# The two products of a level of the attention's inversion handed out as two pieces, with the shares per slot raised by 1.12

## The chip, the cores and the metric

The kernel runs on one core of one Trainium2 chip. The metric is the device time of one execution in microseconds; the median over the runs counts.

## The reference, cut to what matters

Inputs are q, k, v of shape (4, 8, 768, 48), beta of shape (4, 8, 768) and the weights of two mixtures. Three parts follow one another:

```python
# attention with a delta rule, per batch and head, over t = 0 .. 767
y[t] = q[t] @ state
state = state + beta[t] * outer(kn[t], v[t] - state.T @ kn[t])
# first mixture: x is y as 3072 tokens x 384
h = x @ w_in                      # 384 x 2048
x2 = maximum(0.01 * h, h) @ w_out # 2048 x 384
# second mixture, 8 experts, P by 8 rounds of normalising rows and columns
out = sum_e P[:, e] * (maximum(x2 @ w1[e], 0) @ w2[e])   # 384 x 1024 x 384
```

## The kernel before, in words

**Staging.** The 768 positions are cut into 6 steps (t) of 128 positions; a step holds 4 batches (b) of 8 heads. Within a step the recurrence is solved in closed form: part1 normalises k, transposes it and forms the lower triangular matrix of a step (nh and nl are its high and low half in fp16); solve inverts the 32 x 32 diagonal blocks for all batches at once on VectorE (16 x 16 for steps 0 and 1, named in SMALL); part2(t, b) joins the blocks level by level to the inverse of 128 x 128, refines it, and applies it to v and to the state. The first mixture (main_a) then takes the 512 tokens of a step, and the second mixture begins when all six steps are through.

**A level.** For s in (32, 64), and 16 ahead of them in steps 0 and 1, the loop in part2 (L275 on) does: 8 small products of nh and a half of u into a PSUM bank (L284), copies of the result into p by ScalarE (L287), 8 products of x with p (L290) and, for s over 16, 8 products of p with x (L294) into two more banks, and copies of these back into u and x (L297, L300). The second products wait for the copies of the first. A level ends with a yield.

**The order of the work.** part1, solve and part2 are generators; what stands between two yields is a piece. Two queues hold them: bgq has the threads part2(t, b), bgs has part1 and solve. `pump` takes one piece from the next active thread, round robin; the end of a thread counts as one more unit. Main work is also a generator: main_a yields after each third of a first product (L503, three matmuls of 512 columns) and after each of three output chunks of a second product (L555, three matmuls). Each yield is a slot: step 0 has 120, the others 96. At each slot `spend` adds the share of RATES0 (step 0, six equal stretches of slots) or RATES (steps 1 to 4, four stretches) to a credit and pumps one piece for each whole credit: the first number of a triple is for bgq, the second for bgs, the third for pieces of convert, which rewrites the weights of the first mixture. If nothing can be pumped (a part2 waits until solve of its step is done), the credit is cut to 1 and the slot passes.

```python
                ru, rs, rc = rates[n * len(rates) // total]
                bgq.spend(ru, 3)
                bgs.spend(rs, 1)
```

A thread (t, b) starts when (t, b - 2), or (t - 1, b + 2) for b below 2, has ended, so at most two part2 run side by side. Ahead of the first item of the next step, need_x1 pumps bgq until all four threads of that step are through, without main work between, and then transposes their y into x1. Step 0 runs its first LEAD = 4 items on batches 0 and 1 alone, and need_x1 has a stop for batches 2 and 3 after three of them.

**The start.** part2(0, 0) and part2(0, 1) run before main_a, in 14 rounds: one piece of each of the two, one of part1(1) and one of convert. What is left of the three after 14 rounds is run one after the other.

```python
        for _ in range(14):
            run(a0, 1)
            run(a1, 1)
            with tc.issue_after(solved[0].ins):
                run(p1_1, 1)
            run(cv_gen, 1)
        run(a0)
        run(a1)
```

The pieces of part2 in order: two for the products of q and k (m, L256), one for the blocks (L271), one per level, two for the refinement (p, L309 and L311), two for its product with x (u, L321), one for the state's part (ks, L329), w (L337), and y with the new state (L343, L346, L354). The build orders each engine's instructions by their place in the program and by when it takes them to be ready, so the order on an engine can differ from that of the code. Pools: bg has three PSUM banks for the pieces, po three for the second product, ph two for the first.

Of the kernel before, what the change touches and what calls it, by code (L numbers as in the profile page):

```python
# [41 lines left out]

STIR = (145, 20)

RATES0 = ((0.65, 0.3, 0.1), (0.7, 0.5, 0), (0.7, 0.45, 0), (1.05, 0.8, 0.4), (0.7, 0.35, 0), (1.05, 0, 0))
RATES = ((0.7, 0.5, 0), (0.7, 0.5, 0), (0.7, 0.5, 0), (0.7, 0.7, 0))


@with_exitstack
def delta_moe_kernel(ctx: ExitStack, tc: tile.TileContext, k_l, v_l, q_l, beta_l, wa_in, wg, wc, out):  # L50
# [67 lines left out]
    def bank(name):  # L118
        if early is not None and early:
            early[0] += 1  # L120
            i = early[0] % 6
            if i >= 3:
                return po_p.tile([128, 512], F32, tag=f"po{i - 3}", name=name)
        return bg_p.tile([128, 512], F32, tag="bg", name=name)
# [92 lines left out]
    def solve(t):  # L217
        size = 16 if t in SMALL else 32
        nd = 32 // size

        def blocks(x):
            return x[:, 0:nd * size * 33].rearrange("p (d r) -> p d r", d=nd)[:, :, 0:size * 32].rearrange(
                "p d (c i) -> p d c i", c=size)[:, :, :, 0:size]

        ld = a1_p.tile([128, 1056], F16, tag="ld", name="ld")
        dve.transpose(out=ld[:, 0:1024], in_=a_d.rearrange("p a b -> p (a b)"))
        xs = a1_p.tile([128, 1056], F32, tag="xs", name="xs")
        pool.memset(xs, 0.0)
        pool.memset(xs[:, 0:1024:33], 1.0)
        ldb, xsb = blocks(ld), blocks(xs)  # L230
        yield
        for j in range(size - 1):
            m = size - 1 - j
            tm = a1_p.tile([128, 1024], F32, tag="tm", name="tm")
            tv = tm[:, 0:nd * (j + 1) * m].rearrange("p (d c i) -> p d c i", d=nd, c=j + 1)
            xv = xsb[:, :, 0:j + 1, j + 1:]
            dve.tensor_tensor(out=tv, in0=ldb[:, :, j:j + 1, j + 1:].to_broadcast([128, nd, j + 1, m]),  # L237
                              in1=xsb[:, :, 0:j + 1, j:j + 1].to_broadcast([128, nd, j + 1, m]), op=ALU.mult)
            dve.tensor_tensor(out=xv, in0=xv, in1=tv, op=ALU.subtract)
            if j % 2 == 1:  # L240
                yield
        xt = a1_p.tile([128, 32, B * H], F32, tag="tm", name="xt")
        solved.append(dve.transpose(out=xt.rearrange("p a b -> p (a b)"), in_=xs[:, 0:1024]))
        xt_of[t] = xt
        done.add(("xt", t))
        yield

    def part2(t, b):
# [26 lines left out]
        for s in (16, 32, 64) if t in SMALL else (32, 64):  # L275
            pt = p1[b % 2]
            nb = C // (2 * s)

            def half(ap, odd):
                return ap.rearrange("p h (n two s) -> p h n two s", two=2, s=s)[:, :, :, odd, :]  # L280

            ps = bank("l_ps").rearrange("p (h n s) -> p h n s", h=H, n=nb)
            for h in range(H):
                marks.append(pe.matmul(out=ps[:, h], lhsT=nh[:, h, :], rhs=half(u, 1)[:, h], start=True, stop=True))  # L284
            for i in range(nb):
                o = 2 * s * i
                act.activation(out=pt[o:o + s, :, o + s:o + 2 * s], in_=ps[o:o + s, :, i, :], func=ACTF.Copy)  # L287
            ps = bank("l_ps").rearrange("p (h n s) -> p h n s", h=H, n=nb)
            for h in range(H):
                pe.matmul(out=ps[:, h], lhsT=x[:, h, :], rhs=half(pt, 1)[:, h], start=True, stop=True)  # L290
            if s > 16:
                ps2 = bank("l_ps").rearrange("p (h n s) -> p h n s", h=H, n=nb)
                for h in range(H):
                    pe.matmul(out=ps2[:, h], lhsT=pt[:, h, :], rhs=half(x, 0)[:, h], start=True, stop=True)  # L294
            for i in range(nb):
                o = 2 * s * i
                act.activation(out=u[o:o + s, :, o + s:o + 2 * s], in_=ps[o:o + s, :, i, :],  # L297
                               func=ACTF.Copy, scale=-1.0)
                if s > 16:
                    act.activation(out=x[o + s:o + 2 * s, :, o:o + s], in_=ps2[o + s:o + 2 * s, :, i, :],  # L300
                                   func=ACTF.Copy, scale=-1.0)
            if s == 16:
                dve.transpose(out=x.rearrange("p a b -> p (a b)"), in_=u.rearrange("p a b -> p (a b)"))
            yield
# [187 lines left out]
    def step_items(t):  # L492
        n = LEAD if t == 0 else 0
        return ([(t, f, 0, 2) for f in range(n)] + [(t, f, 0, B) for f in range(n, NF1)]
                + [(t, f, 2, B) for f in range(n)])
# [80 lines left out]
    if True:  # L576
# [7 lines left out]
        def load_part2(t, b):  # L584
            def run():
                if (t, b) not in vq:
                    load_vq(t, b)
                yield from part2(t, b)
            return run
# [57 lines left out]
        for t in range(NT - 1):  # L647
            add_step2(t + 1)
            if t + 2 < NT:
                tt = t + 2  # L650
                bgs.add(("p1", tt), lambda tt=tt: part1(tt), after=[("s", t + 1)] + [("p2", t, b) for b in range(B)])
                bgs.add(("s", tt), lambda tt=tt: solve(tt), after=[("p1", tt)] + [("p2", t + 1, b) for b in range(B)])
            rates = RATES if t else RATES0
            total = 6 * len(step_items(t))
# [429 lines left out]
```

## Time and profile before

| what | value |
|---|---|
| runs | 2474.03, 2477.55, 2491.28 us; median 2477.55 us |
| profiled execution | 2491.82 us, its span 2489.8 us |
| mean granted clock of TensorE | 0.963 |
| TensorE matmul, weight loads | 95%, 84% of the span |
| VectorE, ScalarE, GpSimd | 51%, 47%, 38% of the span |

Times within the execution count from the span's start. The x1 transposes, which end a step's attention, stand at 112 and 163 us (the two halves of step 0) and at 315, 449, 588, 724 and 843 us (steps 1 to 5); the second mixture begins at about 945 us. PE is TensorE, PEld its weight loads, DVE VectorE, ACT ScalarE, POOL GpSimd, SP the engine that issues most DMAs. Ends of matmuls are modelled; a row's bracket gives the idle time of the engine before it and who ended it.

### The profile page before, as it was taken

The numbers are of one execution on the slowest core, as the hardware profiler recorded it, in microseconds if no ns is written. First come the engines' busy times: TensorE is split into PE (matmuls) and PEld (weight loads), VectorE is DVE, ScalarE is ACT, GpSimd is POOL, SyncE is SP. The second block draws the span as 40 slices with busy tenths as digits, with TensorE's granted clock in tenths as the row PEclk, the third lists the DMA queues.
The fourth block names the chain that finished last, engine by engine and source line by source line (L and its number), as shares of the span: only waits on it lengthen the run. The fifth ranks groups of instructions, "written<-read, shape, count | busy, mean of one in ns | idle before, by whom it ended". The sixth has DMA issues, their size and how long they took to land.

```text
span 2489.8 us, 35427 instructions
## 1 busy us (share of the span) xinstructions
PE 2374.4 (95%) x13836; PEld 2087.3 (84%) x13836; DVE 1263.4 (51%) x2320; ACT 1162.8 (47%) x2121; POOL 937.5 (38%) x966
## 2 busy tenths in 40 slices
PE   6788899999999999999999999999999999999999
PEld 5776677877877777899999999999999999999998
DVE  8567846446362357644444454444444544444444
ACT  6887666564654544433333344333333443333332
POOL 6435312132322213444434444444444443444441
PEclk7689999989899999999999999999999999999999
DMA  3355552424233552111111131111111311111111
GB/s 117 122 172 181 185 174 94 142 92 142 82 126 129 165 174 76 51 51 46 49 46 51 52 102 51 46 51 51 49 48 51 96 45 51 51 51 46 50 51 38
DMA packets 108695, 214.83 MB, mean 86 GB/s; under 512 B 11504, under 2 KB 79728, under 8 KB 108528
## 3 DMA queue, kind: packets, MB, share of 16 engines
q1 hardware_dynamic: 108528, 212.58, 27.5%
q8 instruction: 108, 1.77, 0.3%
q14 instruction: 59, 0.48, 0.1%
HBM read 190.43 MB, written 22.02 MB: 85 GB/s over the span
## 4 chain that ended last, share of the span: by engine, by line
PE 77%; ACT 10%; DVE 7%; issue 3%; DMA 2%; POOL 2%; SPq 0%; ACTq 0%; POOLq 0%; DVEq 0%
PE ye L964 32%; PE ph L880 13%; PE w L880 5%; PE y L880 5%; PE z L880 5%; PE ph L503 4%; PE po L555 4%; PE y_ps L346 2%; ACT x L271 2%; PE w_ps L337 2%; ACT a_d L205 1%; ACT p L287 1%; PE g_ps L189 1%; ACT u L297 1%; DVE tm L237 1%
## 5 line engine op out<-in xcount | busy, mean ns | idle before, releaser
L745 POOL TENSOR_TENSOR w2l<-stg,w2h 128x768 fp32r<-128x768 f32 x96 | 182.2, 1898 | 454.2 <-ACT w2h L744 454.2
L734 POOL TENSOR_TENSOR w1l<-stg,w1h 128x384 fp32r<-128x384 f32 x192 | 271.4, 1436 | 184.7 <-ACT w1h L733 167.2
L977 DVE SCALAR_TENSOR_TENSOR acc<-ye,pm,acc 128x384 f32<-128x384 f32 x168 | 103.5, 616 | 435.4 <-PE ye L964 435.4
L731 POOL TENSOR_TENSOR stg<-stg 128x128 f32<-128x128 f32 x384 | 209.0, 565 | 305.5 <-DMA stg<-wc 284.5
L890 ACT ACTIVATE xc<-ph 128x512 f32<-128x512 f32 x96 | 57.5, 599 | 448.5 <-PE ph L880 345.3
L555 PE MATMUL po<-gh,w 128*128 128x512 f32 (+1 forms) x600 | 217.3, 406 | 2.9 <-ACT gh L543 2.8
L880 PE MATMUL ph<-xoh,w1h 128*128 128x512 f32 x480 | 193.1, 402 | 4.7 <-DVE q L895 3.1
L503 PE MATMUL ph<-x1h,w 128*128 128x512 f32 (+1 forms) x600 | 186.7, 418 | 8.9 <-DVE leak L541 4.4
L895 DVE TENSOR_TENSOR q<-q,ph 128x512 f32<-128x512 f32 x192 | 132.2, 688 | 121.8 <-PE ph L880 121.8
L880 PE MATMUL ph<-xoh,w1l 128*128 128x512 f32 x480 | 188.1, 392 | 0.0
L880 PE MATMUL ph<-xol,w1h 128*128 128x512 f32 x480 | 187.7, 391 | 0.0
L733 ACT ACTIVATE w1h<-stg 128x384 fp32r<-128x384 f32 x192 | 121.1, 680 | 116.8 <-DMA stg<-wc 82.7
L541 DVE TENSOR_TENSOR leak<-leak,ph 128x512 f32<-128x512 f32 (+1 forms) x100 | 66.3, 663 | 165.7 <-ACT leak L540 165.5
L503 PEld LDWEIGHTS ph<-x1h,w 128*128 128x128 f32 x600 | 113.2, 202 | 32.5 <-DMA w<-wa_scratch 5.9
L555 PEld LDWEIGHTS po<-gh,w 128*128 128x128 f32 x600 | 115.4, 196 | 25.6 <-ACT gh L543 5.5
L545 POOL TENSOR_TENSOR gl<-leak,gh 128x512 fp32r<-128x512 f32 x48 | 62.1, 1294 | 192.4 <-ACT gh L543 174.7
L555 PE MATMUL po<-gl,w 128*128 128x512 f32 (+1 forms) x300 | 120.2, 401 | 3.8 <-POOL gl L545 2.3
L895 DVE TENSOR_TENSOR c<-xc,y 128x512 f32<-128x512 f32 x96 | 66.0, 688 | 106.2 <-PE y L880 83.1
L880 PEld LDWEIGHTS ph<-xoh,w1h 128*128 128x128 f32 x480 | 90.2, 188 | 34.4 <-DVE h31l L909 6.8
L880 PEld LDWEIGHTS ph<-xoh,w1l 128*128 128x128 f32 x480 | 90.2, 188 | 19.5
L540 ACT ACTIVATE leak<-ph 128x512 f32<-128x512 f32 (+1 forms) x100 | 57.8, 578 | 96.5 <-PE ph L503 93.8
L880 PEld LDWEIGHTS ph<-xol,w1h 128*128 128x128 f32 x480 | 90.3, 188 | 14.2
(316 smaller groups left out, 6683.7 us busy)
## 6 DMA issues: line engine op xcount, KB each, us to landing
w<-wa_scratch SPq DMA_DIRECT2D x100, 768.0 KB, 4.3
stg<-wc SPq DMA_DIRECT2D x192, 384.0 KB, 3.3
raw<-wa SPq DMA_DIRECT2D x48, 256.0 KB, 3.0
wa_scratch<-cvp SPq DMA_DIRECT2D x48, 256.0 KB, 2.5
stg<-x_scratch SPq DMA_DIRECT2D x10, 768.0 KB, 4.7
q<-q_l SPq DMA_DIRECT2D x24, 256.0 KB, 2.7
v<-v_l SPq DMA_DIRECT2D x24, 192.0 KB, 2.4
x_scratch<-x2o SPq DMA_DIRECT2D x18, 256.0 KB, 3.8
```

What stands on the lines that cost most here:

```text
L503: pe.matmul(out=ps, lhsT=wt[:, c * 128:(c + 1) * 128], rhs=xx[:, c], start=(n == 0), stop=(n == 3 * KD - 1))
L541: dve.tensor_tensor(out=g, in0=g, in1=ps, op=ALU.max)
L545: (dve if t in (0, 1, NT - 1) else pool).tensor_tensor(out=gl, in0=g, in1=fr(gh), op=ALU.subtract)
L555: pe.matmul(out=po[c][:, cols], lhsT=wt[:, DM + c * 128:DM + (c + 1) * 128], rhs=xx, start=(i == 1 and m == 0), stop=(i == n and m == 2), ...
L731: pool.tensor_tensor(out=s[:, o], in0=s[:, x], in1=s[:, y], op=op)
L733: ordered(act.activation(out=hi[:, j], in_=s[:, i], func=ACTF.Copy))
L734: pool.tensor_tensor(out=lo[:, j], in0=s[:, i], in1=fr(hi[:, j]), op=ALU.subtract)
L745: pool.tensor_tensor(out=lo, in0=s, in1=fr(hi), op=ALU.subtract)
L880: ordered(pe.matmul(out=ps, lhsT=w[:, a], rhs=x[:, b].rearrange("p s k -> p (s k)"), start=first, stop=i == 2 and (a, b) == terms[-1], ski ...
L895: ordered(dve.tensor_tensor(out=c, in0=x, in1=y, op=op))
L964: ordered(pe.matmul(out=ps[:, 0:DM], lhsT=xx[:, o:o + 128], rhs=wt, start=(f == 0 and i == 0), stop=(f == NF2 - 1 and i == 2), skip_group_ ...
L977: dve.scalar_tensor_tensor(out=a, in0=y, scalar=pm[:, t * B + b, e:e + 1], in1=a, op0=ALU.mult, op1=ALU.add)
```

## The change

The level's loop gets a yield between the copies of the first product and the second products, and the first numbers of the triples are raised (0.65 to 0.72, 0.7 to 0.78, 1.05 to 1.15); the shares of bgs and convert stay. Nothing else changes: the same instructions with the same operands.

```diff
-RATES0 = ((0.65, 0.3, 0.1), (0.7, 0.5, 0), (0.7, 0.45, 0), (1.05, 0.8, 0.4), (0.7, 0.35, 0), (1.05, 0, 0))
-RATES = ((0.7, 0.5, 0), (0.7, 0.5, 0), (0.7, 0.5, 0), (0.7, 0.7, 0))
+RATES0 = ((0.72, 0.3, 0.1), (0.78, 0.5, 0), (0.78, 0.45, 0), (1.15, 0.8, 0.4), (0.78, 0.35, 0), (1.15, 0, 0))
+RATES = ((0.78, 0.5, 0), (0.78, 0.5, 0), (0.78, 0.5, 0), (0.78, 0.7, 0))
@@ -285,6 +285,7 @@
             for i in range(nb):
                 o = 2 * s * i
                 act.activation(out=pt[o:o + s, :, o + s:o + 2 * s], in_=ps[o:o + s, :, i, :], func=ACTF.Copy)
+            yield
             ps = bank("l_ps").rearrange("p (h n s) -> p h n s", h=H, n=nb)
             for h in range(H):
                 pe.matmul(out=ps[:, h], lhsT=x[:, h, :], rhs=half(pt, 1)[:, h], start=True, stop=True)
```

## Rows read from the trace of the kernel before

**Rows 1.** The page, busy us (share of the span) xinstructions:
```profile
PE 2374.4 (95%) x13836; PEld 2087.3 (84%) x13836; DVE 1263.4 (51%) x2320; ACT 1162.8 (47%) x2121; POOL 937.5 (38%) x966
```

**Rows 2.** Stretches; busy us (instructions) by engine, granted clock, DMA share, GB/s:
```profile
0.00:164.00 164.00, 121.09 (x984) 107.82 (x985) 117.46 (x299) 118.66 (x264) 78.09 (x97) 0.70 0.44 140
164.00:317.00 153.00, 127.64 (x1009) 105.12 (x1010) 119.03 (x267) 112.92 (x259) 62.75 (x73) 0.91 0.55 177
317.00:591.00 274.00, 256.32 (x1914) 211.99 (x1913) 146.78 (x327) 161.94 (x290) 67.54 (x62) 0.94 0.36 120
591.00:845.00 254.00, 240.96 (x1801) 198.93 (x1800) 96.39 (x192) 136.29 (x251) 69.50 (x62) 0.95 0.36 117
...
945.00:2489.80 1544.80, 1537.23 (x7754) 1395.24 (x7752) 729.07 (x1155) 585.74 (x982) 637.34 (x652) 1.00 0.19 53
```

**Rows 3.** Waits of TensorE in 0:164, then in 164:845 (us, times, longest):
```profile
PE l_ps L290 <- ACT p L287: 9.6, 10, 3.4
...
PE l_ps L290 <- ACT p L287: 18.3, 28, 1.8
```

**Rows 4.** Timeline 480.75 to 485.55, two levels of step 3's threads:
```profile
480.75 0.84 PE L503 MATMUL ph<-x1l,w 128*128 128x512 f32 x3
...
481.43 0.41 PE L284 MATMUL l_ps<-u,nh 128*128 128x64 f16 x8
...
481.67 0.95 PE L503 MATMUL ph<-x1h,w 128*128 128x512 f32 x3
...
482.45 0.40 PE L555 MATMUL po<-gh,w 128*128 128x512 f32 x1
...
482.69 0.41 PE L290 MATMUL l_ps<-p,x 128*128 128x64 f16 x8
...
483.17 0.40 PE L284 MATMUL l_ps<-u,nh 128*128 128x64 f16 x8
...
483.40 0.48 PE L555 MATMUL po<-gl,w 128*128 128x512 f32 x1
...
483.72 0.62 PE L555 MATMUL po<-gh,w 128*128 128x512 f32 x2
...
484.41 0.62 PE L555 MATMUL po<-gh,w 128*128 128x512 f32 x2
484.74 0.76 ACT L287 ACTIVATE p<-l_ps 32x256 f16<-32x256 f32 x2
...
485.55 0.39 PE L290 MATMUL l_ps<-p,x 128*128 128x64 f16 x8 [0.52 <-ACT p L287]
```

**Rows 5.** Timeline of the start, ACT's part of part1(1) and a conversion's pass:
```profile
99.63 1.06 ACT L198 ACTIVATE nh<-a 128x1024 f16<-128x1024 f32 x1
100.59 2.57 ACT L205 ACTIVATE a_d<-a 32x256 f16<-32x256 f32 x4
...
103.18 0.42 ACT L459 ACTIVATE cvp<-cva 128x256 fp32r<-128x256 f32 x1
```

**Rows 6.** Timeline of TensorE at the end of step 1's main loop:
```profile
436.70 1.88 PE L337 MATMUL w_ps<-v,uc 128*128 128x48 f32 x16
...
441.66 1.03 PE L343 MATMUL y_ps<-state,q 112*128 112x96 f32 x8
...
445.10 1.06 PE L343 MATMUL y_ps<-state,q 112*128 112x96 f32 x8
...
448.56 1.04 PE L481 MATMUL x_ps<-ident,y 128*128 128x128 f32 x8
```

**Rows 7.** Stretches at that end and around a fall of the clock, columns as in rows 2:
```profile
436.00:449.00 13.00, 13.00 (x110) 12.61 (x109) 8.04 (x22) 3.95 (x8) 0.00 (x0) 1.00 0.41 132
...
503.80:517.70 13.90, 11.96 (x93) 10.28 (x91) 8.17 (x15) 12.90 (x21) 7.15 (x6) 1.00 0.22 72
517.70:531.40 13.70, 13.70 (x59) 12.83 (x58) 2.85 (x10) 4.92 (x8) 3.94 (x3) 0.50 0.29 91
531.40:545.10 13.70, 13.68 (x103) 11.47 (x104) 4.79 (x13) 6.68 (x12) 4.26 (x4) 1.00 0.23 78
```

## The prediction

> **What bounds the kernel now.** I read the page's busy shares first, then the stretches, then TensorE's waits, and last the timeline of one level. TensorE is busy 95% of the span and no other engine over 51% [rows 1], so the time is TensorE's work plus its idle time. The stretches [rows 2] show where it idles: from 945 us on, in the last mixture, 1537.23 of 1544.80 us are busy at full clock, and nothing of the change is there. Ahead of 845 us, where attention and first mixture are mixed, 164.00 − 121.09 = 42.9 us are idle in 0:164 (before x1 of step 0 is whole), 25.4 in 164:317, 17.7 in 317:591 and 13.0 in 591:845. The change lives in these 99 us.
>
> The waits [rows 3] put a name on part of them. The second product of a level (L290) waits for the copies p of the first (L287): 9.6 us (10 waits) in 0:164 and 18.3 us (28 waits) in 164:845, together 27.9. The timeline [rows 4] shows one wait whole: two L555 begin at 484.41 and need 2 × 0.227 us, so L290 could begin at 484.86; it begins at 485.55, when ACT's L287 ends. Lost are 0.69 us where the row books 0.52, because matmul ends are modelled late. (0.227 is the pitch: three L503 follow 0.68 us after three others all through this loop, as from 480.75 to 481.43.) With 0.16 us more for each, the 38 waits are 27.9 + 6.1 = 34 us: 18.3 + 4.5 = 23 in 164:845 and 9.6 + 1.6 = 11 before.
>
> The same rows show that TensorE's order isn't the order of the code: between L284 and L290 of one piece stand three L503 and one L555. The build's ordering by priority puts main matmuls there already, but too few: the first product at 481.43 lets L290 go at 482.69 (1.3 us), the one at 483.17 only at 485.55 (2.4 us; its copies start at 484.74, since ACT has others to do first).
>
> **The change, part by part.** *The split.* No instruction is added or removed. The later half gets a later place in the hand-out, so a lower priority than the main matmuls of the slots in between. Following the credits through the code: of the 56 levels (8 threads of steps 0 and 1 with three, 16 with two) 6 lie in the start and 50 in the main loops. In 45 of these, two or three slots and one piece of the other thread now stand between the halves, in 3 one slot, in 2 none. A slot is three matmuls, 0.68 us [rows 4]. The other thread's half adds 0.23 us (L284, 483.17 to 483.40) or about twice that (L290 and L294). So 1.6 to 2.5 us stand where 1.3 to 2.4 are needed. Bounds in 164:845: 0 to −23 us. I take three quarters, −17, since the needed time comes near the given one only where ACT is queued.
>
> *The start (0:164).* Here there is little to fill with. Threads (0,0) and (0,1) had 13 pieces and an end, just the 14 rounds; they now have 16, so w and y (L337, L346) fall behind the loop. The other users of a round keep their count: the rest of part1(1) is out by round 10, where the threads were at their u pieces and are now at p; three more conversions stand ahead of w. If all of that delays the chain, part1's last piece costs ACT 1.06 + 2.57 us and three conversions of some four passes of 0.42 us another 5 [rows 5]: +9 us together. On the other side all 11 us of waits could go. The start is one chain of dependent pieces, at a mean clock of 0.70 [rows 2], so a wait removed there mostly becomes the next wait: −11 to +9, and I take 0. The DMAs that these pieces issue (raw, cvp on SP) keep their order, and no queue gets a new wait ahead of them.
>
> *Rates.* A thread of step 2 and later has 15 units instead of 13 (1.15 times), of steps 0 and 1 17 instead of 14 (1.21); the shares rise by 1.10 to 1.12. So a slot gets a little less of the attention done. solve(2) ends at slot 33 of step 1 instead of 27, as its predecessors end at slots 96 and 97 instead of 87 and 89 of step 0. What is undone when the next step's x1 is needed is pumped in one go: for step 2 nine pieces (u0, two u1, ks, w and y of both threads) where there were two y, for steps 3 to 5 three or four (of w, w, y, y) where there were none, none and one; at step 0's first stop 20 instead of 15. The end of step 1's loop shows such a burst as it is now [rows 6]: y, state, y, state follow from 441.66 to 448.56 without a main matmul and without a wait, then x1, and TensorE is busy 13.00 of 13.00 us at full clock [rows 7]. Bounds: 0, if the longer ones run like that, to +27 (the slow rival's price, below). I take +0.5 us for each of four, for y that waits on the copy of w: +2.
>
> *Closer pieces, more changes of kind.* Every other pair of dependent pieces comes 1/0.70 − 1/0.78 = 0.15 slot nearer, 0.1 us. And where a small product ends and main matmuls resume, the first takes 0.32 us (483.40 to 483.72) instead of 0.227. If all 50 halves come to stand alone that is 50 × 0.09 = 4.5 us; at least 0, since many have main matmuls around them already. With the 0.1 us on some other waits I take +3 (bounds 0 to +10). PSUM gains room: a level held three of three bg banks in one piece, now one and then two. The buffer of p is held longer, but belongs to one thread until that ends.
>
> Sum: −17 + 0 + 2 + 3 = −12 us on the profiled execution (2491.82 us around a span of 2489.8), so 2480 there. That execution stands at the upper edge of the runs (2474.03 to 2491.28); against their median 2477.55 the forecast is 2466 us.
>
> **The rivals.**
> *The clock comes back too.* In 164:845 the missing clock of [rows 2] adds up to 2 × (0.09 × 153 + 0.06 × 274 + 0.05 × 254) = 86 us at half rate, worth 43 us. The fall at 517.7 us [rows 7] follows a stretch with 11.96 of 13.90 us busy; in the stretch after the half-rate one, 13.68 of 13.70 are busy and the clock is 1.00. Denser halves would then pay twice: all 34 us of waits and a tenth of the clock (4), less 4 of price, make −34, 2443 us. The Trainium skill ("TensorE: Matmul & The Clock Gate", Part 1: The HAM clock gate) has the slow clock as the default that activity lifts; the trace agrees, in that this fall follows idle time. Against the rival: only a part of those waits lies near a fall of the clock, and the start is a chain.
> *Nothing moves.* The second half is taken as soon as it is ready all the same, or the wait goes to the next reader of u and x (p, L309). Then ±4 us: 2477. For it: the fill of [rows 4]. Against it: 28 waits that the present order does leave.
> *Slower: the bursts fall to half clock.* w and y are products of 48 columns; four step ends now have w, w, y, y back to back, where the y alone took 6.9 us [rows 6]. If each leaves a half-rate stretch as long as that of [rows 7], 13.7 us, it costs 6.9 us, four of them 27; with 5 us won by the split and 3 lost by closer pieces that is +25: 2502. From the third step end on (17/6.9 = 2.5) it eats the gain. Against it: 436:449, with two w and two y in it, ran at 1.00 [rows 7].
>
> **How the numbers follow.** Forecast 0.50 (own range 2453 to 2479), clock 0.20, nothing 0.15, bursts 0.15. About 1% (25 us) is what a measurement of this kernel can tell from no change. Faster by over 1% (below 2453): the clock case and the forecast's edge, 0.20; slower by over 1% (above 2502): the worse half of the bursts and a little of the start's, 0.09; the rest, 0.71, within. The range leaves out the better half of the clock case and the worse half of the bursts: 2443 to 2495.
>
> **What would show it.** Right: L290's wait for L287 falls from 18.3 to some 5 us in 164:845, with two main slots between L284 and L290; the last mixture keeps its 1545 us; x1 of steps 1 to 5 comes 2 to 4 us earlier per step. The start is right if 0:164 keeps its length within 5 us. The burst term is wrong if the granted clock falls around the step ends, or if L503 waits for x1 there. The forecast as a whole is wrong if L290's wait shrinks and TensorE's idle time ahead of 845 us does not.

## The result, and the profile after

The changed kernel takes 2502.78 us (median of 6 runs, 2501.51 to 2507.79) against 2487.95 (6 runs of before on that chip, 2474.03 to 2491.28): the ratio of the two means is 1.0076, 95% interval 1.0051 to 1.0102. It is slower by three quarters of a per cent, where 2466 us were forecast, and lies above the forecast's range. The profiled execution took 2501.51 us around a span of 2499.8, so 10 us of span more than the one of before [rows 1]. That is half of the 19 us between the means of the runs: before's profiled execution is slower than each of its six runs, and after's is its fastest. The stages below explain these 10 us; what the other runs add stands with the experiments.

The page of the kernel after, TensorE's busy row and the row of its granted clock:

```profile
PE 2388.0 (96%) x13836; PEld 2088.5 (84%) x13836; DVE 1266.0 (51%) x2320; ACT 1158.1 (46%) x2121; POOL 937.3 (37%) x966
PEclk7588899998989999999999999999999999999999
```

TensorE has the same 13836 matmuls and is busy for 13.6 us longer. Its idle time is span less busy: 2499.8 − 2388.0 = 111.8 us after and 2489.8 − 2374.4 = 115.4 before. So the change did take idle time away, and the span still grew. What else makes a matmul long is its clock: the mean granted clock was 0.963 before and 0.960 after, and (1 − clock) × span, the cost of running part of the span at half rate, is 92.1 and 100.0 us. So 10.0 = −3.6 (idle) + 7.9 (clock) + 5.7 (the rest, by subtraction: matmuls that got longer at the same clock, as no run shows apart).

The stretches of the kernel after, which answer to [rows 2] (columns as there):

```profile
0.00:166.00 166.00, 124.65 (x985) 109.23 (x985) 114.91 (x293) 116.76 (x259) 76.15 (x93) 0.70 0.40 127
166.00:332.00 166.00, 138.60 (x990) 111.60 (x989) 124.80 (x271) 115.32 (x264) 67.52 (x79) 0.86 0.53 173
332.00:604.00 272.00, 256.01 (x1931) 208.76 (x1930) 148.42 (x329) 160.36 (x294) 65.73 (x60) 0.94 0.37 122
604.00:854.00 250.00, 239.33 (x1801) 195.12 (x1800) 93.28 (x192) 132.60 (x245) 69.53 (x62) 0.96 0.36 119
954.00:2499.80 1545.80, 1538.26 (x7755) 1395.63 (x7753) 729.96 (x1155) 586.00 (x982) 636.18 (x652) 1.00 0.19 53
```

Most of the clock's loss is in the second stretch: 166:332 ran at a clock of 0.86 for 990 matmuls, where 164:317 had 0.91 for nearly as many. The last mixture is what it was (1545.8 us against 1544.8). Cut at the products of x1, the stages are: the start (until x1 of step 0 is made whole) 162.7 us before and 164.7 after; the first loop (from there to x1 of step 1) 152.5 and 165.8; the later loops (to x1 of step 5) 527.6 and 521.6. So +2.0, +13.3, −6.0, and +0.7 behind. Nearly all of the loss is in the first loop; the later loops, where most of the split's gain was expected, did gain, but 6 us and not most of 17.

The waits of TensorE in 0:166, the first row, and in 166:854 of the kernel after, the others, which answer to [rows 3] (us, times, longest; L290 is L291 now, and all lines below it are one higher):

```profile
PE l_ps L291 <- ACT p L287: 2.3, 4, 1.2
...
PE l_ps L291 <- ACT p L287: 11.3, 10, 3.1
PE po L556 <- ACT gh L544: 8.8, 9, 2.0
PE m_ps L256 <- ACT mt L260: 5.5, 5, 2.6
PE kt_ps L180 <- ACT u L298: 4.3, 3, 1.6
PE w_ps L338 <- DVE xs L239: 3.6, 2, 2.2
```

The wait that the split was to remove fell from 18.3 us (28 times) to 11.3 (10 times). Others came: po on gh stood at 2.2 us before, m_ps on mt at 2.7, kt_ps on u at 0; w on L239 is new, and e7 and e12 below show what it costs. Some went: ks on v had 4.5 us before and w on wv 3.7.

How a level looks now, timeline of TensorE in the kernel after, answering to [rows 4]:

```profile
491.85 0.41 PE L284 MATMUL l_ps<-u,nh 128*128 128x64 f16 x8
492.09 0.95 PE L504 MATMUL ph<-x1h,w 128*128 128x512 f32 x3
...
492.88 0.41 PE L284 MATMUL l_ps<-u,nh 128*128 128x64 f16 x8
...
493.90 0.41 PE L291 MATMUL l_ps<-p,x 128*128 128x64 f16 x8
```

Main matmuls and the other thread's first product stand between L284 and L291 now, and L291 begins without a wait. At this level the edit does what it says.

The end of step 2's loop (the burst w, w, y, y in front of x1 of step 3), and w of the next burst, in the kernel after, timeline of TensorE, which answers to [rows 6]; a bracket is the idle time ahead of the row and what ended it:

```profile
578.40 0.94 PE L504 MATMUL ph<-x1h,w 128*128 128x512 f32 x3
581.58 6.68 PE L338 MATMUL w_ps<-v,uc 128*128 128x48 f32 x32 [2.23 <-DVE xs L239]
588.05 1.99 PE L344 MATMUL y_ps<-state,q 112*128 112x96 f32 x8
...
594.74 1.92 PE L344 MATMUL y_ps<-state,q 112*128 112x96 f32 x8
...
601.35 1.57 PE L482 MATMUL x_ps<-ident,y 128*128 128x128 f32 x8
...
720.87 3.54 PE L338 MATMUL w_ps<-v,uc 128*128 128x48 f32 x20 [1.41 <-DVE xs L239]
```

and the two stretches around that wait (columns as in [rows 2]):

```profile
575.20:582.00 6.80, 4.57 (x33) 3.87 (x31) 6.46 (x19) 1.71 (x3) 2.27 (x2) 1.00 0.32 116
582.00:602.50 20.50, 20.50 (x100) 20.50 (x100) 6.38 (x12) 8.53 (x16) 2.34 (x3) 0.50 0.17 46
```

This is the view to remember. Behind a wait of 2.23 us TensorE is busy for 20.50 of 20.50 us, which any column of busy shares calls perfect, and its granted clock is 0.50, the lower of its two levels (1.2 of 2.4 GHz), for all of it: the products of 96 columns take 1.99 us for eight instead of 1.1. The same happens at 720.87 behind 1.41 us, with 20.5 us at half clock from 721.9. What VectorE did meanwhile, timeline of VectorE in the kernel after:

```profile
578.88 0.30 DVE L239 TENSOR_TENSOR xs<-xs,tm 128x135 f32<-128x135 f32 x1
...
580.11 0.25 DVE L239 TENSOR_TENSOR xs<-xs,tm 128x87 f32<-128x87 f32 x1
580.28 0.55 DVE L332 TENSOR_TENSOR v<-v,ks_ps 128x384 f32<-128x384 f32 x1
580.87 0.55 DVE L334 TENSOR_TENSOR v<-v,beta 128x384 f32<-128x384 f32 x1
```

w needs v, and v needs ks, which TensorE had done by 578.4; but the steps of solve for the next steps (L239) stand ahead of L332 on VectorE. The burst is pumped without main work between, so nothing else stands there for TensorE. Nine products L556 could have: gl, the last of their operands to come, is done at 578.33 (GpSimd L546, 1.38 us from 576.95), and yet they follow x1, from 602.68. No run moves them ahead of w.

The kernel before had such places too, two of them, in rows not shown so far (timeline of TensorE in the kernel before):

```profile
516.47 2.55 PE L337 MATMUL w_ps<-v,uc 128*128 128x48 f32 x16 [1.58 <-ACT wv L338]
653.31 2.84 PE L337 MATMUL w_ps<-v,uc 128*128 128x48 f32 x16 [1.60 <-ACT wv L338]
```

The first is what stands ahead of the half-rate stretch of [rows 7] (13.70 us from 517.7); the second is followed by another 13.7 us. So after has two long stretches of 20.5 us in the later loops, where before had two of 13.7. These places were not added but traded; what was added is in the first loop, where no half-rate stretch that begins there is longer than 6.8 us in before and after has three, of 10.2, 13.7 and 10.2 us (from 203, 261 and 309).

### The profile page after: what moved, and what is told of

It reads as the page before. It is cut to its first block, busy times and chain, and to the rows that moved or that the text cites. A ratio compares the mean times of both kernels' runs of the same rounds, so it can differ in the third digit from the quotient of the medians.

```text
span 2499.8 us, 35421 instructions
## 1 busy us (share of the span) xinstructions
PE 2388.0 (96%) x13836; PEld 2088.5 (84%) x13836; DVE 1266.0 (51%) x2320; ACT 1158.1 (46%) x2121; POOL 937.3 (37%) x966
## 4 chain that ended last, share of the span: by engine, by line
PE 79%; ACT 8%; DVE 7%; issue 3%; DMA 2%; POOL 2%; SPq 0%; ACTq 0%; POOLq 0%; DVEq 0%
PE ye L965 32%; PE ph L881 13%; PE w L881 5%; PE y L881 5%; PE z L881 5%; PE po L556 5%; PE ph L504 5%; PE y_ps L347 2%; PE w_ps L338 2%; ACT a_d L205 2%; DVE tm L237 1%; DVE xs L239 1%; PE g_ps L189 1%; ACT x L271 1%; PE y_ps L344 1%
## 5 line engine op out<-in xcount | busy, mean ns | idle before, releaser
L556 PE MATMUL po<-gh,w 128*128 128x512 f32 (+1 forms) x600 | 225.6, 416 | 11.5 <-ACT gh L544 11.4
L504 PE MATMUL ph<-x1h,w 128*128 128x512 f32 (+1 forms) x600 | 180.7, 409 | 5.7 <-DVE leak L542 4.4
L556 PEld LDWEIGHTS po<-gh,w 128*128 128x128 f32 x600 | 115.6, 198 | 34.1 <-ACT gh L544 15.6
L546 POOL TENSOR_TENSOR gl<-leak,gh 128x512 fp32r<-128x512 f32 x48 | 62.2, 1296 | 175.5 <-ACT gh L544 155.1
L556 PE MATMUL po<-gl,w 128*128 128x512 f32 (+1 forms) x300 | 121.6, 407 | 4.3 <-DVE gl L546 2.9
```

The lines of the kernel that those rows point to most:

```text
L504: pe.matmul(out=ps, lhsT=wt[:, c * 128:(c + 1) * 128], rhs=xx[:, c], start=(n == 0), stop=(n == 3 * KD - 1))
L546: (dve if t in (0, 1, NT - 1) else pool).tensor_tensor(out=gl, in0=g, in1=fr(gh), op=ALU.subtract)
L556: pe.matmul(out=po[c][:, cols], lhsT=wt[:, DM + c * 128:DM + (c + 1) * 128], rhs=xx, start=(i == 1 and m == 0), stop=(i == n and m == 2), ...
```

## The experiments

Each kernel had 12 runs (e5 had 7), beside 35 of the kernel before (30 beside e5 to e8). The kernel before had medians of 2483.32, 2485.44, 2480.34 and 2483.63 us in the four groups. The column "clock term" is the mean of (1 − granted clock) × span over all runs of a kernel, in us; the six runs of before beside after have no clock on record, so the row of before has the four groups. "At half clock" is worked out from windows of 1 us: the sum of 2 × (1 − granted clock). Stages are cut as above, from one profiled execution each.

| kernel | ratio (95%) | clock term | start | first loop, at half clock | later loops, at half clock |
|---|---|---|---|---|---|
| before | | 81.2 to 86.5 | 162.7 | 152.5, 27 | 527.6, 58 |
| after | 1.0076 (1.0051 to 1.0102) | 105.5 | 164.7 | 165.8, 48 | 521.6, 51 |
| e1 split alone | 1.0045 (1.0023 to 1.0067) | 93.1 | 163.7 | 173.5, 61 | 501.1, 7 |
| e2 both shares alone | 1.0028 (1.0006 to 1.0051) | 92.5 | 166.1 | 157.7, 51 | 520.3, 38 |
| e3 split, late shares 0.91 | 1.0045 (1.0026 to 1.0064) | 95.8 | 167.3 | 164.6, 53 | 516.0, 38 |
| e4 late split and late shares | 1.0023 (1.0004 to 1.0043) | 88.9 | 162.2 | 151.5, 34 | 518.5, 44 |
| e5 early split alone | 1.0063 (1.0038 to 1.0087) | 98.9 | 167.2 | 173.8, 67 | 515.9, 38 |
| e6 late split alone | 0.9956 (0.9936 to 0.9975) | 76.0 | 167.1 | 152.4, 35 | 504.0, 7 |
| e7 after, solve behind v | 1.0034 (1.0017 to 1.0052) | 92.2 | 168.6 | 163.8, 54 | 512.5, 27 |
| e8 e4, solve behind v | 0.9984 (0.9967 to 1.0002) | 78.5 | 159.0 | 147.6, 31 | 519.2, 31 |
| e9 split of step 1 alone | 1.0012 (0.9987 to 1.0037) | 83.8 | 163.1 | 154.6, 31 | 513.4, 34 |
| e10 split of step 0 alone | 1.0044 (1.0021 to 1.0067) | 89.2 | 166.8 | 159.4, 48 | 520.9, 44 |
| e11 late shares alone | 0.9951 (0.9932 to 0.997) | 74.4 | 165.4 | 151.8, 34 | 502.6, 10 |
| e12 after, filled | 1.0055 (1.0035 to 1.0075) | 95.4 | 166.9 | 160.0, 41 | 516.5, 31 |
| e13 early shares alone | 1.0023 (1.0 to 1.0046) | 95.8 | 166.9 | 166.0, 72 | 518.2, 41 |
| e14 early shares × 0.9, late shares | 1.0027 (1.0004 to 1.005) | 90.0 | 166.4 | 162.9, 55 | 509.5, 7 |
| e15 late shares, solve behind v | 0.9986 (0.9962 to 1.001) | 77.5 | 164.4 | 150.8, 27 | 516.4, 24 |
| e16 late shares 0.86 | 1.0054 (1.0029 to 1.0078) | 92.6 | 160.9 | 150.7, 32 | 537.6, 61 |

The clock term settles what the loss is made of. Mean time less clock term is 2398.4 us for after and 2397.2 to 2400.0 for the four groups of before: over the runs the whole loss is clock. For all 18 kernels this rest lies between 2394 and 2406 us, while the clock term goes from 74 to 106. It also varies from run to run of one and the same program: over the 135 runs of before from 67 to 100 us, and their times from 2469 to 2497. So a single profile, with its stages, is one draw: before's, at 92 us, is a bad one, e13's (2501.55 us) and e5's (2508.09) are the slowest of their runs, and a stage counts where several kernels agree. The first loop does: 160.0 to 165.8 us in the four kernels with both early edits (after, e3, e7, e12), 147.6 to 152.5 in the seven with neither (before, e4, e6, e8, e11, e15, e16).

Read the last columns against each other next. The later loops take 501 to 504 us where 7 to 10 us of them are at half clock, 516 to 521 where 37 to 44 are, and 537.6 where 61 are; the first loop takes 148 to 155 at 27 to 35 us and 158 to 174 at 41 to 72. Half of each microsecond at half clock is lost: from e1 to e16 that is 27 of the 36.5 us by which their later loops differ, and idle time is another 12 (25.9 us in e1, 38.3 in e16), together the difference to within 3 us. Where a row stands off this line (e8, e14, e15), it is by idle time too (34.6, 33.2 and 35.8 us). The idle time of the whole span lies between 110 and 117 us in the kernels after, e5, e6, e11, e13 and before, while (1 − clock) × span of the same profiles goes from 74 (e11) to 110 us (e13).

**The two parts apart, and a larger share (e1, e2, e3).** The first question was which edit costs the time, and whether more share in the later steps, which shortens the bursts at their ends, takes it back.

e1:
```diff
+            yield
```


> The split alone, with the shares of before. Theory burst (the loss sits at the step ends, where w, w, y, y of two threads run without main matmuls between and TensorE falls to half clock): the bursts grow to 17, 10, 10 and 11 units at the ends of steps 1 to 4, so it is slower than the changed kernel, 2510 to 2525, with half-clock stretches of 10 to 20 us at all four of these ends. Theory step 0 (the loss sits in the first loop, where 1.12 times the pieces per slot crowd ScalarE and the main copies gh come late): with the old shares the loop of step 0 falls back to some 153 us and the time to 2485 to 2492. Either way L290's wait for L287 stays at half of before.

e2:
```diff
-RATES0 = ((0.65, 0.3, 0.1), (0.7, 0.5, 0), ...
+RATES0 = ((0.72, 0.3, 0.1), (0.78, 0.5, 0), ...
-RATES = ((0.7, 0.5, 0), ...
+RATES = ((0.78, 0.5, 0), ...
```


> The shares alone, without the split. Theory burst: no burst is left at the ends of steps 1 to 4 (0 units each), the half-clock stretches there stay away, the time is that of before or up to 8 us less: 2478 to 2490. Theory step 0: the denser pieces cost in the first loop with or without the split: loop of step 0 at 160 to 166 us, time 2495 to 2502. L290's wait stays at 25 to 30 us in either.

e3 (the split and RATES0 of the change):
```diff
-RATES = ((0.78, 0.5, 0), ...
+RATES = ((0.91, 0.5, 0), ...
```


> The split with RATES0 of the change and RATES raised to 0.91 instead of 0.78, so that the bursts are 5 units at the end of step 1 and none at steps 2 to 4. Theory burst: the two half-clock stretches of 20.5 us at the ends of steps 2 and 3 go, 20 us less than the changed kernel: 2480 to 2486. Theory step 0: the first loop keeps its 166 us and all else changes little: 2496 to 2503.

Measured: 2492.88 us (2488.13 to 2501.96), 2489.87 (2481.55 to 2497.77) and 2494.27. Each part alone is slower than before, each by less than the whole (for e1 the intervals overlap). e1 is the surprise: bursts of 17, 10, 10 and 11 pieces at the step ends, far longer than in the change, and yet the later loops are the shortest of all (501.1 us, 7 at half clock). So the length of a burst is not what costs. Its loss is in the first loop, 21 us. e3 keeps one long stretch, 17.1 us behind a wait of 1.6 us ahead of w, so a larger share doesn't cure it either.

**Early and late halves (e4, e5, e6, e9, e10).** The first loop belongs to steps 0 and 1, so the split was made for some steps only.

e4 (RATES of the change, RATES0 of before), and e6 with both shares of before:
```diff
+            if t >= 2:
+                yield
```


> The split only for steps 2 to 5, RATES0 as before, RATES as changed: start and first loop are those of before. Theory step 0: the 13 us of the first loop come back, 2486 to 2491, with x1 of step 1 near 315 us. Theory burst: the step ends keep their half-clock stretches, the time stays within 5 us of the changed kernel, 2497 to 2505.

> The split only for steps 2 to 5, shares of before, bursts of 12, 10, 10 and 11 units. Theory: where the split has main matmuls to put between the halves it pays, as L290's wait there is worth some 13 us of 18 and large bursts did no harm in the split alone (no half clock at its step ends): ratio 0.992 to 0.998, x1 of step 1 to the second mixture 595 us instead of 612. Rival, any burst costs: 1.002 to 1.010, with half-clock stretches of 15 to 20 us at two or more step ends.

e5, and with `t == 1` e9, with `t == 0` e10, all with the shares of before:
```diff
+            if t < 2:
+                yield
```


> The split only for steps 0 and 1, shares of before. If the split's price lies in the start and the first loop (more waits over 1 us there, and with them more time at half clock), this kernel keeps the whole price of the split alone: ratio 1.004 to 1.008, x1 of step 1 at 328 us or later instead of 315. If it lies at the ends of the later loops, it is at before: 0.998 to 1.002.

> The split for step 1's threads alone (they run in the first loop), shares of before. If the price of the early split (ratio 1.0063 for steps 0 and 1) lies in the first loop, where a wait ahead of ks and w let the clock fall for 30 us, it is all here: 1.004 to 1.007, loop of step 0 165 us or more instead of 152. If it comes from the start and step 0's second half: 0.999 to 1.002.

> The split for step 0's threads alone (the start, and batches 2 and 3 in the first items), shares of before. The counterpart of the run before: 0.999 to 1.002 by the first theory, 1.004 to 1.007 by the second, then with 0:164 at 168 us or more.

Measured: e4 2488.6 us, e5 2499.63, e6 2471.13 (2467.9 to 2482.23), e9 2481.27, e10 2487.74 (2482.23 to 2504.67). The late split alone makes the kernel faster by 0.44%, and the early split alone makes it slower by 0.63%; of that, step 0's share is +0.44%, and step 1's can't be told from none. e5 shows the costly stretch of the first loop, timeline and window:

```profile
241.03 1.73 PE L331 MATMUL ks_ps<-state,kT 112*128 112x96 f32 x8 [1.50 <-DVE v L333]
...
243.16 3.65 PE L339 MATMUL w_ps<-v,uc 128*128 128x48 f32 x16
```

```profile
241.40:272.10 30.70, 30.70 (x136) 28.27 (x136) 12.80 (x35) 17.56 (x36) 8.81 (x10) 0.50 0.44 133
```

A wait of 1.50 us, then ks, w, w, y, y, and TensorE is busy 30.70 of 30.70 us at the lower level. And e4, which ought to be e6 plus a little, is slower than e6; it has the wait of after again (timeline and window of e4), and e8 below takes it away:

```profile
563.30 5.16 PE L339 MATMUL w_ps<-v,uc 128*128 128x48 f32 x32 [2.25 <-DVE xs L239]
```

```profile
565.40:585.90 20.50, 20.50 (x96) 20.01 (x96) 6.55 (x10) 9.58 (x17) 2.35 (x3) 0.50 0.16 46
```

**Is it the wait on solve? (e7, e8, e12)** If the 2.23 us of L239 ahead of w set off the stretch, then solve's instructions placed behind the scaling of v of the step before must remove it; and if the wait is filled with other products, it must go too, without any change to VectorE.

e7 (the changed kernel) and e8 (e4) with:
```diff
+    v_done = {}
+    def solve_behind(t):
+        g = solve(t)
+        while True:
+            with tc.issue_after(v_done[t - 1].ins):
+                if next(g, "end") == "end":
+                    return
+            yield
-        (pool if t < 2 and (b + t) % 4 == 0 else dve).tensor_tensor(out=v, in0=v, in1=bb, op=ALU.mult)
+        eng = pool if t < 2 and (b + t) % 4 == 0 else dve
+        scaled = eng.tensor_tensor(out=v, in0=v, in1=bb, op=ALU.mult)
+        if eng is dve:
+            v_done[t] = scaled
```


> The changed kernel with VectorE's instructions of solve(t) issued behind the scaling of v of step t - 1's last thread, so that no block step of solve (L239) stands between ks and w in a burst. Theory: TensorE's wait of 2.2 and 1.4 us ahead of w at the ends of steps 2 and 3, which the two half-clock stretches of 20.5 us follow, goes and the stretches with it: 12 to 20 us less than the changed kernel, 2483 to 2491. Rival, the row of small products itself lowers the clock: the stretches stay, 2499 to 2506. Later solves could delay the next step's part2 by some us in either case.

> Split for steps 2 to 5 only, RATES0 of before, RATES as changed, and solve behind the scaling of v as in the run before. Theory: against the same kernel without the last edit (2488.6, half-clock stretches of 20.5 and 17.1 us at two step ends) 12 to 18 us less: 2471 to 2477, ratio 0.994 to 0.998. Rival: 2486 to 2491.

e12 (the changed kernel) with twenty products whose result is not read, behind ks of thread 3 in steps 3 and 4:
```diff
+            if t in (3, 4) and b == 3:
+                ps = bank("stir_ps")
+                for _ in range(20):
+                    pe.matmul(out=ps[:, 0:256], lhsT=stir[:, 0:128], rhs=stir, start=True, stop=True)
```


> The changed kernel with 20 idle products of 256 columns behind ks of batch 3 in steps 3 and 4, whose results nothing reads; they stand just where TensorE waits 2.2 and 1.4 us ahead of the row w, w, y, y. Theory, the wait lowers the clock and the row of small products keeps it low: the products cost at most 2 x 2.2 us, less the idle time that they fill, and the two half-clock stretches of 20.5 us go: 10 to 20 us less than the changed kernel, 2483 to 2493. Rival, the row itself lowers the clock: the stretches stay, and the time is that of the changed kernel or 1 to 3 us more, 2501 to 2508.

Measured: e7 2492.78 us, some 10 less than after (ratios 1.0034 and 1.0076, from two groups); e8 2480.22, 8.4 less than e4; e12 2496.53. Each lies between the range of the theory and that of the rival. The clock term of all runs fell by 13.3 us from after to e7 and by 10.4 from e4 to e8. The burst of e7, timeline of TensorE, and the window around it:

```profile
581.55 3.67 PE L351 MATMUL w_ps<-v,uc 128*128 128x48 f32 x32
585.06 1.10 PE L357 MATMUL y_ps<-state,q 112*128 112x96 f32 x8
...
592.03 1.04 PE L495 MATMUL x_ps<-ident,y 128*128 128x128 f32 x8
```

```profile
566.00:594.00 28.00, 28.00 (x235) 24.33 (x234) 13.37 (x31) 12.00 (x23) 6.33 (x6) 1.00 0.37 118
```

The same products in the same order, without the wait: from w to x1 10.5 us (592.03 − 581.55), where after took 19.8 (601.35 − 581.58), and the clock is 1.00 throughout. That is the cleanest pair of the study. The gain in total stays smaller than two such places would give; waits of other readers grew in 332:845 (waits of TensorE in e7):

```profile
PE ph L517 <- DVE leak L555: 8.2, 4, 2.2
PE l_ps L294 <- DVE u L283: 7.4, 4, 2.9
```

e12 confirms half of it. Timeline of TensorE and two stretches in e12:

```profile
577.81 2.35 PE L337 MATMUL stir_ps<-stir 128*128 128x256 f16 x20
...
580.94 3.74 PE L342 MATMUL w_ps<-v,uc 128*128 128x48 f32 x32
584.52 1.10 PE L348 MATMUL y_ps<-state,q 112*128 112x96 f32 x8
...
586.65 3.45 PE L351 MATMUL y_ps<-wv,mt 128*128 128x48 f32 x16 [1.03 <-ACT wv L343]
```

```profile
580.10:586.90 6.80, 5.69 (x46) 5.07 (x45) 3.93 (x10) 3.29 (x6) 1.14 (x2) 1.00 0.21 58
586.90:600.60 13.70, 13.70 (x68) 13.52 (x68) 5.58 (x9) 7.02 (x13) 1.27 (x1) 0.50 0.15 39
```

Filled, the 32 products w run at full clock (3.74 us, 6.68 in after). Then y waits 1.03 us for the copy of w, and now the stretch begins there, 13.7 us of it. The stretch from 721.9 in after is gone in e12. By its time e12 can't be told from after (1.0055 and 1.0076, with intervals that overlap); its clock term is 10.1 us lower.

**Shares alone, early and late (e11, e13 to e16).**

e11 is RATES of e2 alone, e13 RATES0 of e2 alone, e15 is e11 with the edit of e7. e14 and e16:
```diff
-RATES0 = ((0.65, 0.3, 0.1), (0.7, 0.5, 0), ...
+RATES0 = ((0.585, 0.3, 0.1), (0.63, 0.5, 0), ...
```
(e14, with RATES of e11)
```diff
-RATES = ((0.7, 0.5, 0), ...
+RATES = ((0.86, 0.5, 0), ...
```
(e16, RATES0 of before)

> No split, RATES0 of before, RATES as changed. Theory: the raised shares move the place where ks and w of the last threads meet solve's block steps and the end of a burst, with or without the split; 1.001 to 1.005, a fall of the clock of 13 us or more at w of one or two loops. Rival, the shares cost only with the split (late split: 0.9956 with the old, 1.0023 with the new): 0.998 to 1.001.

> RATES0 as changed, RATES of before, no split. Theory, the terms add: RATES0 costs what both shares cost less what RATES gains, 1.0028 + 0.0049, so 1.005 to 1.010, with the extra time in the first loop (x1 of step 1 at 320 us or later instead of 315). Rival, the shares cost only in company: 0.998 to 1.002.

> No split, RATES as changed, RATES0 lowered to 0.9 of before. Theory, a crowded first loop is what costs, less crowding gains: 0.990 to 0.995 against 0.9951 with RATES0 of before. Rival, any move of the pieces of the first loop shuffles its waits, and before was a good place: 0.996 to 1.003.

> RATES alone, with solve behind the scaling of v. The trace of RATES alone has no wait ahead of w in the later loops, so by the theory that this edit helps only where solve stands between ks and w there is nothing to win: 0.994 to 0.998. Rival, the edit helps by itself: 0.990 to 0.992.

> RATES alone, raised to 0.86 instead of 0.78. If the gain comes from ending the attention ahead of the need (no burst) it stays: 0.993 to 0.997. If it comes from where the last ks and w happen to meet VectorE's and ScalarE's other work, it can go: 0.998 to 1.003, with waits over 1.3 us ahead of w in one or two loops.

Measured: e11 2467.73 us (2464.36 to 2474.39), e13 2488.45, e14 2490.02, e15 2480.02, e16 2496.78. e11 is the fastest kernel of the study, against the theory that the late shares cost time. So the loss of e2 lies with the early ones: with them the kernel goes from 0.9951 (e11) to 1.0028 (e2). Alone (e13) they cost 0.23%, at the edge of no change and less than the 0.5 to 1.0% that were expected. Windows of the later loops of e11, e6 and before:

```profile
317.00:820.00 503.00, 473.92 (x3718) 390.17 (x3717) 242.16 (x521) 295.76 (x539) 136.09 (x123) 0.99 0.38 124
```

```profile
319.50:823.50 504.00, 474.73 (x3722) 384.87 (x3721) 248.54 (x521) 295.62 (x539) 137.67 (x124) 0.99 0.37 125
```

```profile
315.00:843.00 528.00, 497.29 (x3717) 411.25 (x3717) 244.34 (x522) 298.21 (x540) 137.04 (x124) 0.95 0.36 120
```

Idle are 29.1, 29.3 and 30.7 us: nearly the same. In these executions the gain of 24 us is the busy time at a clock of 0.99 instead of 0.95; over the runs e6 gains 11.5 us, with 10.5 less of clock term, and e11 12.2, with 6.8. And the waits of the level in e11 and e6 (319:822 and 321:826) say that the split's own purpose has next to no part in it:

```profile
PE l_ps L290 <- ACT p L287: 11.7, 23, 1.1
```

```profile
PE l_ps L292 <- ACT p L287: 2.9, 3, 1.4
```

e6 removed most of that wait, e11 left most of it, and both take the same time, and neither profile has the waits of before ahead of w (1.58 and 1.60 us). The two gains do not add: together they are e4, +0.23%, with waits of 2.25 and 1.41 us ahead of w again. More share does not go on helping: e16, at 0.86, has three long stretches and is slower by 0.54%, more than either range expected. The first of them begins behind this row (timeline of e16):

```profile
498.73 2.63 PE L337 MATMUL w_ps<-v,uc 128*128 128x48 f32 x16 [1.17 <-DVE v L333]
```

Solve's place helps where solve was the wait (e7, e8) and brought nothing where it was not (e15, 0.9986, against e11, 0.9951, with intervals that just overlap). With the late shares, early shares cost in both directions (e2 up, e14 down, against e11).

**Where a wait is not needed, or not enough.** Two rows of the first loop speak against a rule that a wait must stand right ahead. Timeline of TensorE in e13, and a window:

```profile
296.48 0.39 PE L555 MATMUL po<-gh,w 128*128 128x512 f32 x1
296.70 0.40 PE L503 MATMUL ph<-x1h,w 128*128 128x512 f32 x1
...
300.56 1.99 PE L343 MATMUL y_ps<-state,q 112*128 112x96 f32 x8
```

```profile
297.10:300.50 3.40, 3.40 (x33) 3.40 (x32) 2.58 (x8) 1.11 (x3) 0.33 (x1) 0.98 0.22 54
300.50:317.60 17.10, 17.10 (x75) 16.30 (x75) 6.02 (x17) 3.27 (x8) 1.45 (x2) 0.50 0.43 155
```

TensorE is never idle there, and the clock falls behind 32 products w all the same; in after it does so at 308.9, for 10.2 us. In the later loops it was never so: of their 18 stretches of 10 us or more, over all kernels, each begins behind a wait of 0.84 to 2.25 us ahead of ks, w or y. The other way round it holds less often. The same profiles have 41 such waits of 0.84 us or more: within 4 us behind them the clock fell for 10 us or more 18 times, for 3.4 or 6.8 us 13 times, and not at all 10 times. Behind 203 such waits ahead of other products it fell 60 times, never for as long. A wait of 1.57 or 1.58 us ahead of w led to 13.7 us at half clock in before (516.47), to 6.8 in e9 (515.21) and to 3.4 in e5 (535.99). So, in the later loops, a wait ahead of a row of small products is where a long fall can begin; what decides whether it does is open.

## Why the prediction was wrong

Two steps failed. The sum has no term for TensorE's clock, and over the runs the clock made the whole loss: the clock term is 105.5 us after and 81 to 86 before. And it has no price for the first loop, which got 13.3 us longer in the profile, and longer in every profile with an early edit. Besides, 10 of the 37 us between 2466 and 2502.78 are the base: 2477.55 was the median of three runs, that of six is 2487.95.

**The split.** −17 us in 164:845 was the sum's largest term, mis-sized. The reading of the view was right: main slots stand between L284 and L291, and L291's wait for L287 fell, but by 7 us (18.3 to 11.3), not to some 5. Other readers of ACT's copies took part of it over (po on gh, m_ps on mt, kt_ps on u; +13.7 us together), and as some waits went, the idle time ahead of 845 us moved by 3.6 in all. That was the rival "nothing moves" in part, and the test the text itself named came out against the forecast: that idle time hardly shrank.

**The start.** 0, with bounds −11 to +9: +2.0 us in the profile (164.7 for 162.7). The term held for that stretch, and so did its reason: L290's wait fell from 9.6 to 2.3 us there and the idle time only by some 2. The step that failed is that step 0's further levels, in the loop behind it, were taken to cost nothing: the first loop lost 13.3 us, of which the time at half clock (48 us, not 27) makes 10. Splitting step 0 alone costs 0.44% (e10) and RATES0 alone 0.23% (e13), the latter at the edge of no change, with the first loop at 48 and 72 us of half clock. Falls there stand behind waits of several kinds: in e13 17.1 us behind 2.15 us ahead of w, in after 10.2 us behind 3.12 us ahead of L291. Why the pieces of step 0 put the waits of the first loop at worse places is not settled; no run isolates it.

**The bursts.** +2 was taken, by the one burst in view, 436:449 at clock 1.00 [rows 7]; the rival had 27. The rival had two of four right: the step ends at 582.0 and 721.9 fell to half clock for 20.5 us, 10 us each where it had 6.9. Its cause was not: e1, with far longer bursts, has none in its later loops. And since the two places of before went, the later loops' time at half clock did not grow (58 and 51 us); that the rival's 2502 is the time measured is chance. Without these two places the change would have cost some 10 us less (e7). What the step missed is what stands ahead of w: it looked at the queue on TensorE, and costed the waits inside a burst at +0.5 us, and did not look at VectorE, where solve's steps now stand ahead of v − ks in the burst. A wait of 2.23 us can cost more than 2.23 us if it stands ahead of 20 us of small products.

**The clock.** The forecast had no term for it, only a rival in which it comes back. The fall at 517.7 was read as one that "follows idle time"; the wait of 1.58 us ahead of w (516.47) was not looked up. With it, the stretch's 6.9 us would have been a term that either late edit can remove: the profiles of e6 and e11 have neither place, and over the runs both gained about the 12 us that the forecast promised, mostly for a reason that it did not give. The Trainium skill ("TensorE: Matmul & The Clock Gate", Part 1: The HAM clock gate) has the clock set by how busy TensorE has recently been; here it stayed at half rate through 20.50 us that the profile books as wholly busy, so the busy share of a stretch doesn't say that the clock will rise.

**Closer pieces.** +3 (0 to +10); the rest of the accounting is +5.7. In size roughly right, if all of that rest is theirs; no run shows that it is.

**Range and chances.** The range left out the worse half of the bursts' rival, the one mechanism whose price stood in the trace, and had no case for the first loop, whose mean clock of 0.91 over 164:317 [rows 2] showed falls there too. The first would have carried it past 2495; the second, at 13.3 us, only from 2466 to 2479.

## What to carry to other kernels

Where TensorE bounds a kernel, take the span apart as idle time, (1 − granted clock) × span, and the rest before costing any wait, and over more than one run: here the clock term of one program spread over 33 us, and its mean went from 74 to 106 us over the versions while all else stayed within 12. A wait of 1 to 2 us ahead of a row of small products can cost 5 to 10 us more than its length (18 of 41 were followed by 10.2 to 20.5 us at half clock), so look first for what stands on the other engines ahead of the operand of such a row (here solve ahead of v on VectorE). Two edits of an order, each a gain, may be a loss together (−0.49% and −0.44% gave +0.23%), so each needs its own run; here the late shares alone (0.9951) or the late split alone (0.9956) are the versions to keep.

## What was not expected of the hardware

The same row of products w, w, y, y up to x1 takes 10.5 us at the upper level and 19.8 at the lower (e7 and after), and stretches at the lower that begin at such products last 13.7 to 30.7 us, though TensorE is never idle in them: 582.0 in after, 241.4 in e5, 517.7 in before. But for the two of 13.7 us in before, all stretches in the later loops of before, e6 and e11 lasted 3.4 or 6.8 us. Two falls in the first loop came with no wait at all right ahead of them (e13 at 300.5, after at 308.9). And the granted clock differs from run to run of one program: from 0.960 to 0.973 over the 135 runs of before.
